# A new order, new engine choices and new buffer slots for a two-layer attention and MLP program

## The chip, the cores and the metric

The kernel runs on one core of a Trainium2 chip. The metric is the device time of one execution in microseconds. Of the core's engines, TensorE (PE, with its weight loads PEld) multiplies matrices into PSUM; VectorE (DVE), ScalarE (ACT) and GpSimd (POOL) do the elementwise work; SyncE (SP) issues DMAs. Each engine takes its own instructions in the order in which the program emits them, and waits on semaphores for the others.

## The reference

Two layers, each an attention part A and an MLP part B, both added to the residual, on x of 2048 rows by 512, all bfloat16:

```python
def A(x, wqkv, w_phi, wo):          # 32 heads of 16
    q, k, v = heads(x @ wqkv)
    pq, pk = q @ w_phi, k @ w_phi                     # per head
    phi_q = concat(softmax(pq), softmax(-pq))         # 32 features
    phi_k = concat(softmax(pk), softmax(-pk))
    kv, z = phi_k.T @ v, phi_k.sum(rows)
    o = (phi_q @ kv) / (phi_q @ z + 1e-6)
    return merge(o) @ wo
def B(x, W_gate, W_up, W_down):     # 512 -> 1376 -> 512
    return (relu(x @ W_gate) * (x @ W_up)) @ W_down
for _ in range(2):
    x = x + A(layernorm(x), ...)
    x = x + B(layernorm(x), ...)
```

## The kernel before

The 2048 rows are 16 tiles of 128. Everything stays on the chip: the residual X, the weights, and 21 buffers `ek` for exponentials. The program is a list of 1880 operations (`op`), each with an engine, what it waits for, and the buffers that it takes. An operation may have an alternative on another engine (`alt`).

At the start the key and query weights are multiplied by w_phi on PE ("fold", L448), after turning them: wk by PE (L440), wq by DMA transposes on SP (L435). In each layer a tile then goes through these steps; the line is that of the profile.

- Attention norm: statistics (L477), aggregate (L478), two small activations, scaling (L495), and a transpose to xnTA, by DMA on SP (L461) or by PE (L466) with a copy (L425).
- Keys: K on PE (L535), two exponentials (L538), V on PE (L541) with a copy to vext (L425 on ScalarE, L426 on VectorE), sums of 16 (L546), their reciprocal by two activations (L555, L558), the scaling of ek in two halves (L509, on VectorE or GpSimd), and the key-value sums on PE (L570), which all 16 tiles add into one PSUM tile.
- Queries: Q (L597), exponentials (L600), sums (L603), reciprocal (L606, L608), scaling in two halves (L509), and a DMA transpose to fq on SP (L611).
- Attention: R from the key-value sums (L582, L587), then per tile L622 on PE into the PSUM tile q, a reciprocal (L631 on VectorE, or L629 and L633 on ScalarE), L636, a transpose to oT, the projection (L645), and the residual (L649).
- MLP: centring (L665), square sum (L671 or L673), transpose to xnTB, the last columns of gate and up (L698), gate and up (L722) with relu (L726) and the product (L739 directly from PSUM, or L741 and L730), the down projection (L762), the residual (L769). The tiles go in blocks of 1 to 4. The output is stored by SP (L833).

No scheduler runs when the kernel is built: `arrange` reads the order from a list of numbers, and tables that were found offline say the rest. `PLACE` has a digit for each operation with an alternative (1: take it), `SLOTS` the buffer that each taking operation gets, `ORDER` the numbers of the operations in the order of emission, and `IDLE` how many dummy matmuls stand ahead of each PE operation. `arrange` asserts that an operation comes after those it depends on and that a buffer is free.

Of the kernel before, what the change touches and what calls it, by code (L numbers as in the profile page):

```python
# [142 lines left out]
class K:  # L143
# [9 lines left out]
    "0101110100000000001100000100110001000011010001111000000011001101010101001001001000101001111111011010"  # L153
    "1011110000000100000001001101000000000111011001011111010111000101001100000101111101001100001101010100"
    "1111111110101010010001000011000100000000101100101010100001001100011100010000110011001101000110111001"
    "010110010110111001110100110100000"
)
SLOTS = (
    "0001425210034050000151131234202310332121143404550125d3104c02302b3020a12113g533004002394131703202e141"
    "5i022124504f013k03583226105214413624335a011h100b033c05053623122j214910170400020501131002000245011020"  # L160
    "2500001142021002010100203200101143020002012105002004314023104g13300215112012320410311e34110200400450"
    "10205113120513d5100i42221240121321402422031200151030231042100142131004133610104f33242541002510104203"
    "51101520500512052130201550414201515300804024k2232c4020121152143124212004023502a533344112050010024104"
    "02024213011055002220j4203h05133317362b222f1506242i013a114023391638231c343e352k221d014g10011500020514"
    "0010124302000012011021450000121302100024010021050012201000011011521101530431102000005112025421011101"
    "0213125200125020013101050032154203115143114220221100253415210511200211401013403005210402213013222420"
    "500210300512431510432512113015114024105320310110512400202"
)
IDLE = (
    0, 0, 0, 0, 0, 0, 0, 0, 0, 0, 2, 0, 4, 0, 0, 0, 0, 0, 0, 0, 0,  # L170
# [11 lines left out]
    0, 24, 16, 3, 25, 17, 18, 20, 1, 4, 29, 22, 19, 21, 23, 26, 2, 5, 28, 6, 7, 46, 8, 9, 47, 48, 10, 49, 30, 50,  # L182
    11, 27, 32, 31, 36, 12, 51, 34, 37, 38, 13, 33, 39, 44, 35, 40, 14, 45, 42, 64, 15, 52, 82, 322, 43, 56, 41,
    100, 53, 65, 83, 57, 324, 101, 118, 102, 84, 120, 103, 66, 85, 54, 323, 104, 67, 86, 55, 105, 68, 87, 106, 119,
    121, 69, 58, 325, 122, 110, 70, 123, 88, 217, 71, 111, 124, 59, 89, 125, 60, 250, 72, 126, 61, 73, 252, 92, 90,
    76, 62, 91, 74, 93, 139, 253, 107, 251, 77, 184, 75, 127, 78, 219, 63, 254, 108, 80, 326, 186, 330, 255, 109,
    328, 256, 332, 331, 79, 187, 112, 329, 128, 333, 257, 113, 185, 81, 114, 94, 258, 188, 131, 129, 116, 130, 143,
    327, 95, 115, 271, 132, 151, 96, 140, 259, 189, 144, 97, 218, 220, 133, 221, 117, 222, 141, 98, 142, 153, 134,
    135, 190, 99, 191, 275, 137, 154, 145, 192, 272, 276, 223, 146, 205, 152, 363, 283, 147, 155, 193, 273, 148,
    285, 260, 156, 274, 284, 157, 364, 149, 286, 354, 277, 287, 261, 263, 288, 365, 158, 356, 289, 159, 150, 290,  # L190
    278, 206, 264, 262, 279, 355, 224, 209, 291, 281, 265, 207, 208, 194, 280, 210, 266, 225, 197, 267, 211, 195,
    268, 196, 173, 316, 198, 199, 269, 212, 161, 174, 213, 172, 136, 175, 176, 321, 200, 214, 162, 178, 138, 320,
    163, 296, 318, 201, 215, 179, 293, 317, 180, 297, 203, 166, 304, 216, 294, 292, 227, 181, 177, 295, 238, 336,
    167, 319, 298, 228, 182, 160, 168, 229, 305, 226, 337, 202, 408, 299, 169, 232, 306, 338, 282, 183, 300, 170,
    410, 339, 453, 233, 307, 302, 239, 234, 454, 310, 340, 345, 455, 235, 341, 366, 311, 240, 381, 342, 347, 230,
    456, 312, 382, 236, 367, 444, 241, 357, 231, 314, 270, 368, 445, 204, 308, 244, 457, 369, 358, 458, 346, 237,
    372, 383, 309, 370, 245, 446, 164, 343, 373, 371, 301, 374, 242, 246, 313, 409, 303, 165, 248, 375, 435, 359,
    344, 315, 247, 436, 243, 390, 437, 348, 360, 171, 376, 391, 249, 399, 377, 335, 392, 361, 349, 471, 379, 334,
    401, 362, 350, 384, 400, 426, 351, 473, 480, 472, 462, 352, 481, 427, 378, 353, 482, 417, 428, 483, 464, 429,
    418, 484, 380, 485, 463, 447, 486, 430, 385, 431, 419, 433, 488, 487, 448, 386, 489, 449, 490, 590, 587, 387,  # L200
    491, 588, 589, 496, 432, 492, 497, 598, 493, 388, 434, 498, 402, 599, 600, 389, 494, 499, 601, 403, 591, 602,
    595, 404, 495, 500, 406, 596, 614, 501, 502, 638, 597, 503, 603, 613, 635, 592, 405, 509, 605, 636, 504, 604,
    593, 393, 510, 637, 511, 608, 606, 512, 407, 643, 610, 609, 394, 594, 607, 644, 513, 395, 645, 611, 646, 474,
    396, 514, 515, 656, 661, 648, 397, 516, 657, 658, 507, 475, 659, 612, 517, 451, 476, 651, 477, 438, 647, 653,
    508, 439, 398, 505, 440, 450, 687, 441, 649, 652, 452, 506, 615, 650, 459, 684, 654, 662, 688, 683, 655, 520,
    685, 411, 686, 522, 663, 523, 660, 412, 521, 524, 413, 616, 414, 525, 764, 664, 617, 415, 526, 518, 618, 527,
    528, 478, 416, 695, 465, 705, 697, 479, 519, 466, 710, 707, 529, 761, 711, 760, 530, 712, 762, 619, 689, 639,
    696, 620, 442, 713, 640, 621, 690, 467, 420, 692, 698, 706, 763, 693, 699, 421, 694, 422, 535, 714, 708, 700,
    424, 536, 537, 720, 691, 538, 701, 702, 641, 622, 443, 423, 531, 703, 709, 642, 533, 704, 623, 460, 721, 665,
    425, 468, 725, 666, 722, 469, 461, 667, 627, 534, 668, 669, 532, 769, 470, 715, 670, 628, 765, 716, 717, 767,  # L210
    766, 671, 539, 770, 718, 624, 771, 540, 541, 772, 768, 719, 726, 542, 625, 773, 626, 723, 543, 629, 672, 675,
    724, 630, 673, 631, 729, 777, 674, 633, 676, 774, 778, 632, 544, 775, 677, 546, 545, 678, 548, 780, 679, 549,
    550, 910, 681, 825, 782, 551, 680, 815, 827, 547, 816, 817, 776, 779, 913, 826, 909, 830, 730, 911, 818, 781,
    828, 912, 819, 552, 727, 783, 553, 554, 795, 784, 829, 728, 796, 555, 797, 731, 556, 561, 800, 798, 562, 563,
    801, 799, 732, 802, 564, 733, 820, 734, 803, 805, 735, 822, 804, 736, 737, 557, 807, 559, 558, 806, 915, 914,
    560, 821, 918, 919, 916, 917, 808, 752, 920, 823, 921, 741, 809, 753, 824, 922, 810, 742, 811, 812, 749, 813,
    926, 814, 750, 565, 751, 929, 566, 567, 927, 754, 934, 931, 568, 755, 930, 936, 569, 756, 944, 757, 932, 574,
    933, 946, 785, 758, 575, 576, 577, 786, 787, 923, 788, 572, 924, 789, 925, 928, 790, 573, 979, 791, 1062, 792,
    578, 570, 579, 793, 580, 581, 945, 571, 582, 634, 935, 947, 1063, 1058, 759, 1059, 937, 738, 1060, 1064, 794,
    948, 938, 682, 1061, 739, 835, 1065, 1066, 740, 949, 743, 836, 951, 744, 831, 745, 746, 959, 747, 960, 961, 832,  # L220
    962, 843, 963, 969, 950, 971, 833, 952, 954, 834, 955, 953, 847, 956, 848, 974, 957, 975, 958, 976, 839, 977,
    978, 837, 840, 838, 844, 849, 850, 841, 851, 852, 845, 853, 854, 583, 842, 855, 846, 1070, 584, 1090, 1072, 880,
    1067, 1136, 1092, 585, 1135, 1068, 881, 878, 867, 1069, 586, 1095, 856, 879, 868, 1137, 1140, 882, 970, 1139,
    883, 857, 1141, 1071, 884, 972, 858, 869, 1091, 1142, 861, 748, 870, 973, 1143, 1093, 862, 863, 1073, 939, 871,
    864, 940, 941, 1094, 1074, 872, 964, 865, 873, 965, 874, 966, 942, 875, 1080, 943, 967, 1138, 885, 876, 980,
    1082, 968, 886, 992, 877, 1075, 1144, 1077, 1076, 1145, 1146, 887, 1078, 1079, 890, 888, 889, 1100, 891, 892,
    988, 984, 893, 894, 981, 895, 896, 985, 897, 982, 986, 983, 989, 987, 993, 996, 998, 990, 997, 999, 994, 1000,
    991, 1001, 1096, 1002, 995, 1147, 1027, 1152, 1172, 1029, 1149, 1028, 1003, 1148, 1154, 1030, 1004, 1031, 1153,
# [650 lines left out]
```

## Time and profile before

| what | before |
|---|---|
| median of three runs | 377.24 us (377.06 to 377.68) |
| span of the profiled execution | 375.3 us |
| the median less the span | 1.9 us |
| PE busy | 364.6 us, 97% |
| VectorE busy | 285.1 us, 596 instructions |
| ScalarE busy | 209.7 us, 553 instructions |
| GpSimd busy | 93.5 us, 91 instructions |
| granted TensorE clock | 1.00 |

The span runs from the first to the last instruction of the profiled execution; the time of a run has some 2 us more around it. The profile gives no time of its own for that execution beside the span. Busy times add up what lies side by side on different engines. An instruction's duration is longer than its spacing to the next one, since they overlap in the engine's pipeline: sums are made with the spacing. Line numbers are those of the kernel before; after the change all lines behind the tables are three lower.

### The profile page before, as it was taken

What the parts mean: (1) busy time and instruction counts of PE and PEld (TensorE: products, weight loads), DVE (VectorE), ACT (ScalarE), POOL (GpSimd) and SP (SyncE); (2) the same over time, 40 slices, a digit from 0 to 9 for tenths busy, and PEclk for the clock granted to TensorE, in tenths of its full rate; (3) what the DMA queues carried; (4) which work ended last, traced back from release to release, by engine and by line L of the source; (5) the groups of instructions that cost most, each with busy time, mean ns of one, the idle gap of its engine ahead of it and who ended that gap; (6) DMA issues with size and microseconds to landing.
All of it is one profiled execution on the core that took longest, in us unless ns stands there. A gap on an engine that the chain in (4) does not pass through costs nothing.

```text
span 375.3 us, 7459 instructions
## 1 busy us (share of the span) xinstructions
PE 364.6 (97%) x2793; PEld 216.6 (58%) x2833; DVE 285.1 (76%) x596; ACT 209.7 (56%) x553; POOL 93.5 (25%) x91
## 2 busy tenths in 40 slices
PE   8989997999999999999999999999999999999996
PEld 4534454868554554466476555587745444558585
DVE  6999999999998673685767999999994755543322
ACT  6989999746464532265155499973425323414031
POOL 0377984341010102001004269774000000000000
PEclk9999999999999999999999999999999999999999
DMA  8858844769814221012020102968664120211110
GB/s 256 191 139 175 312 58 85 123 113 132 164 36 84 47 53 31 11 25 56 9 56 2 29 2 57 141 93 142 143 132 85 31 56 2 56 29 51 42 51 30
DMA packets 93444, 31.21 MB, mean 83 GB/s; under 512 B 85248, under 2 KB 92384, under 8 KB 93408
## 3 DMA queue, kind: packets, MB, share of 16 engines
q1 hardware_dynamic: 92992, 30.34, 39.5%
q8 instruction: 22, 0.36, 0.4%
q10 hardware_dynamic: 416, 0.39, 0.3%
q14 instruction: 14, 0.11, 0.1%
HBM read 7.91 MB, written 2.10 MB: 27 GB/s over the span
## 4 chain that ended last, share of the span: by engine, by line
PE 90%; ACT 6%; DVE 1%; POOL 1%; issue 1%; DVEq 0%; another core or an unknown queue 0%
PE b L722 37%; PE b L762 20%; PE b L645 7%; PE b L541 6%; PE b L535 6%; PE b L597 6%; PE b L698 3%; PE q L622 2%; PE q L570 2%; ACT ek L600 1%; POOL ek L509 1%; ACT ek L538 1%; PE q L419 1%; DVE sq L603 1%; ACT hT L425 1%
## 5 line engine op out<-in xcount | busy, mean ns | idle before, releaser
L722 PE MATMUL b<-xnTB,wgu 128*128 128x128 bf16 (+2 forms) x1200 | 149.6, 279 | 0.0
L722 PEld LDWEIGHTS <-wgu 128*128 128x128 bf16 x1200 | 97.1, 98 | 43.6
L509 POOL TENSOR_TENSOR ek<-ek,sk 128x512 bf16<-128x512 bf16 x47 | 51.0, 1109 | 135.5 <-ACT sk L558 108.2
L726 ACT ACTIVATE gu<-b 128x512 bf16<-128x512 f32 (+1 forms) x83 | 47.8, 580 | 64.9 <-PE b L722 64.6
L762 PE MATMUL b<-wd,hT 128*128 128x512 bf16 (+2 forms) x350 | 81.3, 372 | 0.7
L762 PEld LDWEIGHTS <-hT 128*128 128x128 bf16 (+1 forms) x363 | 34.6, 98 | 35.9 <-DVE hT L739 0.2
L509 POOL TENSOR_TENSOR ek<-ek,sq 128x512 bf16<-128x512 bf16 x38 | 42.0, 1127 | 32.6 <-ACT sq L608 18.0
L739 DVE TENSOR_TENSOR hT<-gu,b 128x512 bf16<-128x512 bf16 (+1 forms) x44 | 29.6, 676 | 18.5 <-PE b L722 16.9
L546 DVE TENSOR_REDUCE sk<-ek 128x64 f32<-128x1024 bf16 x32 | 38.7, 1210 | 5.3 <-ACT ek L538 5.2
L538 ACT ACTIVATE ek<-b 128x512 bf16<-128x512 f32 x64 | 35.9, 598 | 9.2 <-PE b L535 8.0
L603 DVE TENSOR_REDUCE sq<-ek 128x64 f32<-128x1024 bf16 x32 | 38.2, 1207 | 0.3 <-POOL ek L509 0.3
L600 ACT ACTIVATE ek<-b 128x512 bf16<-128x512 f32 x64 | 36.1, 623 | 0.6 <-PE b L597 0.5
L730 DVE TENSOR_TENSOR hT<-gu 128x512 bf16<-128x512 bf16 (+1 forms) x39 | 16.7, 429 | 22.5 <-ACT gu L741 22.3
L769 DVE SCALAR_TENSOR_TENSOR X<-b,rsB,X 128x512 bf16<-128x512 f32 (+1 forms) x33 | 23.2, 726 | 13.5 <-PE b L762 13.4
L645 PE MATMUL b<-wo,oT 128*128 128x512 bf16 x118 | 31.2, 379 | 1.2 <-ACT oT L425 0.7
L535 PE MATMUL b<-Wk,xnTA 128*128 128x512 bf16 x122 | 31.4, 379 | 0.3
L541 PE MATMUL b<-wv,xnTA 128*128 128x512 bf16 x124 | 31.0, 379 | 0.4 <-ACT xnTA L425 0.2
L597 PE MATMUL b<-Wq,xnTA 128*128 128x512 bf16 x121 | 30.5, 379 | 0.3
L741 ACT CAST gu<-b 128x512 bf16<-128x512 f32 (+1 forms) x39 | 21.7, 558 | 15.0 <-PE b L722 14.6
L649 DVE SCALAR_TENSOR_TENSOR X<-b,X 128x512 bf16<-128x512 f32 x32 | 21.8, 682 | 3.5 <-PE b L645 3.4
L636 DVE TENSOR_TENSOR o<-q,rd 128x512 bf16<-128x512 f32 x32 | 21.9, 685 | 0.8 <-ACT rd L633 0.6
L477 DVE BATCH_NORM_STATS2 bstA<-X 128x6 f32<-128x512 bf16 x32 | 21.0, 681 | 1.9 <-DMA X<-in_A_x_dram 1.8
(71 smaller groups left out, 349.1 us busy)
## 6 DMA issues: line engine op xcount, KB each, us to landing
out_dram<-X SPq DMA_DIRECT2D x15, 128.0 KB, 1.7
X<-in_A_x_dram SPq DMA_DIRECT2D x6, 256.0 KB, 4.8
wgu<-in_B_W_gate_dram SPq DMA_DIRECT2D x4, 344.0 KB, 4.0
wgu<-in_B_W_up_dram SPq DMA_DIRECT2D x4, 344.0 KB, 3.6
wd<-in_B_W_down_dram SPq DMA_DIRECT2D x5, 256.0 KB, 3.6
wv<-in_A_wqkv_dram SPq DMA_DIRECT2D x2, 256.0 KB, 4.3
wo<-in_A_wo_dram SPq DMA_DIRECT2D x4, 128.0 KB, 3.2
fq<-ek SPq DMA_TRANSPOSE x32, 3.3
```

The source lines that it names most:

```text
L509: e.tensor_tensor(out=out().rearrange("p g s (h f) -> p (g s h) f", f=DH)[:, lo:lo + n], in0=ek.t[:].rearrange("p g s (h f) -> p (g s h) f ...
L535: k = op("PE", mm(4, 512), due, lambda: [nc.tensor.matmul(kp.t[:], lhsT=xnTA[c][:, i, b, :], rhs=Wk2[:, b, :], start=(b == 0), stop=(b == ...
L538: e = [op("ACT", act(512), due, lambda s=s: nc.scalar.activation(out=ek.t[:, :, s, :], in_=kp.t[:].rearrange("p (g e) -> p g e", e=GQ), fu ...
L541: v = op("PE", mm(4, 512), due_v, lambda: [nc.tensor.matmul(vp.t[:], lhsT=xnTA[c][:, i, b, :], rhs=wv[:, b, :], start=(b == 0), stop=(b == ...
L546: a = op("DVE", SUM16, due, lambda: nc.vector.tensor_reduce(out=sk.t[:, row, :], in_=ek.t[:].rearrange("p g s (h f) -> p (g s h) f", f=DH) ...
L597: q = op("PE", mm(4, 512), due, lambda: [nc.tensor.matmul(qp.t[:], lhsT=xnTA[c][:, i, b, :], rhs=Wq2[:, b, :], start=(b == 0), stop=(b == ...
L600: e = [op("ACT", act(512), due, lambda s=s: nc.scalar.activation(out=ek.t[:, :, s, :], in_=qp.t[:].rearrange("p (g e) -> p g e", e=GQ), fu ...
L603: a = op("DVE", SUM16, due, lambda: nc.vector.tensor_reduce(out=sq.t[:], in_=ek.t[:].rearrange("p g s (h f) -> p (g s h) f", f=DH), axis=A ...
L645: a = op("PE", mm(4, 512), due + 3, lambda j=j, yp=yp: [nc.tensor.matmul(yp.t[:], lhsT=oT.t[:, j, b, :], rhs=wo[:, b, :], start=(b == 0), ...
L722: nc.tensor.matmul(ps.t[:, q * W:(q + 1) * W].rearrange("p (i t) -> p i t", t=P), lhsT=wgu[:, s, b, g * P:(g + 1) * P], rhs=xT.t[:, 0:n, b ...
L726: nc.scalar.activation(out=gu.t[:, 0, 0:cols], in_=gp.t[:, 0:cols], func=AF.Relu)
L762: nc.tensor.matmul(yp.t[:, 0:c1 - c0], lhsT=h.t[:m, f * W + i * P:f * W + (i + 1) * P], rhs=wd[:m, f, c0:c1], start=(f == 0), stop=(f == N ...
```

## The change

Only the four tables are replaced, all else is the same text. They were found anew on a model of the machine that knows a lock between the SBUF ports of VectorE and GpSimd and takes all events in order of time. The diff, cut:

```diff
 PLACE = (
-    "0101110100000000001100000100110001000011010001111000000011001101010101001001001000101001111111011010"
...
+    "0101010100000000001100000000111000000110100010001000000000010100000000000001000000000000000010001010"
...
 IDLE = (
-    0, 0, 0, 0, 0, 0, 0, 0, 0, 0, 2, 0, 4, 0, 0, 0, 0, 0, 0, 0, 0,
+    0, 2, 0, 1, 0, 0, 0, 0, 3, 0,
...
 ORDER = (
-    0, 24, 16, 3, 25, 17, 18, 20, 1, 4, 29, 22, 19, 21, 23, 26, 2, 5, 28, 6, 7, 46, 8, 9, 47, 48, 10, 49, 30, 50,
...
+    0, 3, 25, 20, 18, 19, 24, 2, 17, 16, 4, 21, 29, 9, 26, 8, 22, 23, 1, 28, 7, 10, 46, 14, 47, 30, 48, 322, 32, 49,
...
```

Numbers 3 to 15 are loads, 322 to 325 the DMA transposes of wq, 29 the warming matmuls, 30, 32, 34 and 36 the turning of wk. What the tables mean on the engines, counted in the two built programs:

| operation | before | after |
|---|---|---|
| key scaling halves (L509) | VectorE 17, GpSimd 47 | VectorE 20, GpSimd 44 |
| query scaling halves (L509) | VectorE 26, GpSimd 38 | VectorE 12, GpSimd 52 |
| value copies | VectorE 13, ScalarE 19 | VectorE 7, ScalarE 25 |
| gate times up | L739 44, L741 and L730 39 | L739 39, L741 and L730 44 |
| reciprocals in attention | VectorE 17, ScalarE 15 | VectorE 14, ScalarE 18 |
| square sums | VectorE 11, ScalarE 21 | VectorE 8, ScalarE 24 |
| folded weight copies | VectorE 2, ScalarE 6 | VectorE 1, ScalarE 7 |

PE has the same operations, in another order: ahead of the first key-value sums (L570) stand 4 V, 4 K and 4 folds before, and 6 V, 7 K and all 8 folds after; five queries of the second layer stand in the middle of the first layer's MLP. On SP the wq transposes stand among the loads of X instead of behind them, and two of the late weight loads stand ahead of the last X loads.

## The prediction

> **What bounds the kernel now.** I read the page's busy shares and slices first, then PE's waits, then the timeline around the longest of them, then VectorE's groups.
>
> ```profile
> PE 364.6 (97%) x2793; PEld 216.6 (58%) x2833; DVE 285.1 (76%) x596; ACT 209.7 (56%) x553; POOL 93.5 (25%) x91
> ...
> PE   8989997999999999999999999999999999999996
> ...
> DVE  6999999999998673685767999999994755543322
> ACT  6989999746464532265155499973425323414031
> POOL 0377984341010102001004269774000000000000
> PEclk9999999999999999999999999999999999999999
> ```
>
> PE is the wall, but a busy PE need not run at its peak, so I counted its work. Matmuls with nothing between them start 0.216 us apart for 512 columns, 0.109 for 256, 0.083 for 192, 0.056 for 128 and 0.032 for the 65 and 68 wide ones: 1187, 422, 128, 584 and 512 of them make 256.4 + 46.0 + 10.6 + 32.7 + 16.4 = 362 us, dummies included. The rest of the 375.3 is PE's delay: the time at which a group starts less the PE work issued before it. Read off the timeline, the delay is 1.3 us at the first matmul, 4.9 at 13 us, 7.2 at 28 us, 9.8 at 64 us and 10.1 at 365 us. Two stretches make the last 4.9 us, and nothing after 64 us makes more than 0.3. Between 14 and 64 us PE waited for:
>
> ```profile
> PE q L570 <- POOL ek L509: 1.5, 3, 0.7
> PE b L466 <- DVE xn L665: 0.8, 1, 0.8
> PE b L645 <- ACT oT L425: 0.7, 1, 0.7
> PE q L622 <- DVE o L636: 0.2, 1, 0.2
> PE b L466 <- DVE o L636: 0.2, 1, 0.2
> ```
>
> The first line is 18 to 25 us (start gaps 2.3 us in all): key-value sums whose scaled keys GpSimd has not finished. The others are 59 to 64 us (2.6 us): the first tile's way from attention to the MLP.
>
> ```profile
> 59.75 2.33 DVE L603 TENSOR_REDUCE sq<-ek 128x64 f32<-128x1024 bf16 x2
> 59.88 0.40 PE L466 MATMUL b<-ident,o 128*128 128x128 bf16 x4 [0.17 <-DVE o L636]
> 60.95 1.04 PE L645 MATMUL b<-wo,oT 128*128 128x512 bf16 x4 [0.68 <-ACT oT L425]
> ...
> 62.77 0.35 DVE L665 TENSOR_SCALAR xn<-X,rowsum 128x512 bf16<-128x512 bf16 x1
> ...
> 63.18 0.40 PE L466 MATMUL b<-ident,xn 128*128 128x128 bf16 x4 [0.84 <-DVE xn L665]
> ...
> 63.77 0.42 PE L622 MATMUL q<-R,fq 128*128 128x68 bf16 x8 [0.20 <-DVE o L636]
> ```
>
> VectorE runs two L603 reductions for later queries while PE needs it for the first tile. Its groups from 5 to 63 us show 1.3 us idle in all, so what it finishes when is the sum of what is queued ahead:
>
> ```profile
> L546 DVE TENSOR_REDUCE sk<-ek 128x64 f32<-128x1024 bf16 x16 | 19.3, 1209 | 0.1
> L603 DVE TENSOR_REDUCE sq<-ek 128x64 f32<-128x1024 bf16 x9 | 10.6, 1206 | 0.0
> ...
> L509 DVE TENSOR_TENSOR ek<-ek,sq 128x512 bf16<-128x512 bf16 x4 | 3.2, 816 | 0.0
> ```
>
> **The change part by part.** The operations are the same 1880, and PE's are the same to the matmul (six dummies in both), so PE's 362 us stay. Moved are engines, places in the queues, and buffers.
>
> *Engine choices.* Counted in the two built programs: query scalings (L509) on VectorE 26 to 12, on GpSimd 38 to 52; key scalings on VectorE 17 to 20, on GpSimd 47 to 44; value copies (L426/L425) on VectorE 13 to 7, on ScalarE 19 to 25; up-projections read directly by VectorE 44 to 39; three reciprocals, three square sums and one weight copy leave VectorE as well. By spacings in this trace (0.60 us for a 512-wide product, reading or copy, 0.34 for the L730 product, 0.27 for a reciprocal, 0.61 for a square sum) VectorE sheds 11 x 0.60 + 6 x 0.60 + 5 x (0.60 - 0.34) + 3 x 0.27 + 3 x 0.61 + 0.60 = 14.7 us. ScalarE gains 6 + 5 + 1 readings at 0.48, three pairs at 0.22 and three square sums at 0.63: 8.3 us. GpSimd gains 11 x 1.02 = 11.2 us. None of this is a saving by itself; it counts where PE waits.
>
> *Order before 64 us.* I take the third L622 group, which waits for the second tile's L636. VectorE's queue up to that L636, before: 16 statistics x 0.60, 16 aggregates x 0.09, 16 normalisations x 0.32, 25 reductions x 1.13, 20 products and copies x 0.60, one L649 and L665 0.87, small ones 1.1: 58.4 us. Measured end 63.7, so VectorE's own start and idling are 5.2 us. PE has 54.0 us of work before it, and 58.4 + 5.2 + 0.1 - 54.0 = 9.7, the delay that the trace shows (9.8). After: 24 reductions and 16 products and copies, since one L603, three value copies and a weight copy stand later or elsewhere: 54.9 us, against 54.2 of PE. With the same 5.2 the delay is 6.0. The first L622 asks more: VectorE's sum through L582 and L587 is 49.9 against PE's 48.7, and with the 5.0 us that VectorE had idled by then the delay is 6.3.
>
> *ScalarE.* The first L722 group needs the L425 copy of xnTB: sum ahead 54.6 before, 51.9 after (25 query exponentials stand ahead of it, not 32). ScalarE's start and idling were 9.4 us there; kept whole, the delay would be 51.9 + 9.4 + 0.1 - 54.4 = 7.0. Part of that idling was waiting for VectorE's reductions, so 7.0 is the upper end.
>
> *Bare latency.* With every engine free, the first tile's path still takes L645 1.03, L649 0.69 and L665 0.35, and PE has 1.9 us of other work there after the change and 1.1 before; the copy to xnTB (0.6 behind 0.4 us of transposes) leaves 0.3 us uncovered in both. So 6.3 plus 0.3 to 0.6. Between 6.3 and 7.0 I take 6.9, the ScalarE end being the nearer row. What is late next is then PE itself.
>
> *Start.* ScalarE's table load (1.28 us) now stands ahead of its weight load, a Wq fold (L448) stands ahead of the first K and waits for a DMA transpose, and on SP the Wq transposes stand among the X loads, while the load of tiles 14 and 15 waits behind an xnTA transpose. Before, such a transpose landed 4.0 us after issue; now the first is eighth on SP, issued near 0.7 + 7 x 0.53 = 4.5 us, and lands near 9, and PE is held until about 10 anyway by the Wk copies, then by tile 3 (L495 near 10.3). K71 comes at about 12.9 with 7.7 us of PE work ahead, delay 5.2 (4.9 before). Tiles 14 and 15 land near 19 to 20 us, their statistics come up near 21.5. A gain below 4.9 is not to be had here, a loss of 1 us is.
>
> *Key-value sums.* The first L570 stands after 17.8 us of PE work instead of 12.6; GpSimd's first product then starts near 15.3 (14.5 before), and at the closest L570 its sum is 11.6 us under PE's; with the 16.2 us that GpSimd had lost at 25 us before, that asks for a delay of 4.6. The 2.3 us wait goes; the 6.3 above takes its place in part.
>
> *From 64 us.* PE had nothing to give back there, so this part can only lose. Five second-layer query groups stand at 97 to 160 us of PE work (none before 207 in the old order), and at the first L622 of the second layer VectorE's sum less PE's falls from 188.2 - 224.7 = -36.5 to 180.4 - 226.4 = -46.0, so it has 9 us more room there. I cost it at nothing; the cover is that room, and it is gone if a single bank or buffer is short (first rival).
>
> Sum: 9.8 - 6.9 = 2.9 us off the 375.3 us span, 372.4. The runs' median is 1.9 us above the span: 374.3.
>
> **GpSimd and the port.** Beside VectorE's L509, GpSimd's products stretch:
>
> ```profile
> 37.67 6.06 POOL L509 TENSOR_TENSOR ek<-ek,sk 128x512 bf16<-128x512 bf16 x5 [0.39 <-ACT sk L558]
> 41.12 0.68 DVE L509 TENSOR_TENSOR ek<-ek,sk 128x512 bf16<-128x512 bf16 x1
> ```
>
> Five undisturbed ones take 5.1 us; 16 of 85 ran over 1.1 us, up to 1.57, 5 us together. The Trainium skill, page "SBUF — State Buffer", section "Who interferes with whom", says that a VectorE instruction with two SBUF inputs and a GpSimd one that reads SBUF exclude each other, the later one blocking whole; the trace agrees (1.57 against 1.06). By it the stretch should shrink, VectorE having 32 such L509 instead of 43. Against the change speaks "GPSIMD Engine Reference", section "Engine selection": elementwise products belong on VectorE, GpSimd being about twice as slow. The trace agrees on the price, 1.02 against 0.60 us; by that rule alone 14 moved products would cost 14 x 0.42 = 5.9 us.
>
> **Rivals.**
> *Narrow banks.* Six PSUM banks pass between PE and its readers. Counting PE work between a bank's last matmul and its next use, less the reader's 0.60 us and 0.2 of signalling, 15 places behind 64 us have under 0.1 us to spare, 2 before. If ScalarE is in a 0.48 us instruction at four in ten of them, that is 15 x 0.4 x 0.48 = 2.9 us: the gain is eaten, 377.2. For it: ScalarE has 8 us more to do. Against: outside 215 to 265 us it is 35 to 60% busy, and a free ScalarE takes the reader at once.
> *GpSimd late (slower).* The first L622 needs transposed queries behind 28.3 us of GpSimd work. Before, GpSimd reached that sum with 21.4 us of start, idling and stretch: 49.7, plus 3.3 for the DMA transpose, 53.0. PE comes at 48.7 + 6.3 = 55.0. Room 2.0 us. If the products nearly all meet the lock, 14 more at 0.5 us make 60.0, a delay of 11.3 against 9.8, and 378.7. It decides when GpSimd loses 2 us more than before, and it is a loss from 5.5 us more. For it: 11 more products, packed. Against: fewer two-input products on VectorE, and GpSimd waits less, its reductions being earlier in VectorE's queue. The engine-selection rule points here.
> *Better.* ScalarE's idling shrinks with VectorE's queue and the start costs nothing: delay 5.7, 373.1.
> That the change does not do what it says is excluded by the built queues.
>
> **Chances.** Forecast 0.64 (own range 373.4 to 375.8), better 0.06, narrow banks 0.15, GpSimd or the start late 0.15. Three runs spread by 0.16%, so 0.2%, 0.75 us, is what can be told from no change. Faster: 0.64 + 0.06 and 0.06 of the banks' case, 0.76. Same 0.08, slower 0.16. Range 373.0 to 377.6: it leaves out the far ends of GpSimd late and better.
>
> **What would show it.** Right: PE's delay 5 to 5.5 at 13 us, no L570 wait on GpSimd between 18 and 25, about 6.9 when the first L722 starts (near 61.5 us), flat after that. Wrong: L622 or L645 waits near 55 us naming the DMA fq or GpSimd; L722 waits on ScalarE after 64 us; a delay over 7 already at 15 us.

## The result, and the profile after

The changed kernel takes 376.37 us (median of 20 runs, 375.47 to 377.99), the old one beside it 377.53 (20 runs, 376.99 to 377.74): a ratio of 0.9978, 95% interval 0.9969 to 0.9986. It is faster by 1.16 us, where 2.9 had been forecast. The profiled execution took 375.65 us (span 373.5); the old one's span was 375.3.

Lines of the changed kernel's own profile are three lower than those of the kernel before (L506 is the old L509). The experiments from e3 on were written in the old layout and have the old numbers. First the page:

```profile
PE 364.0 (97%) x2787; PEld 216.4 (58%) x2833; DVE 272.3 (73%) x569; ACT 211.7 (57%) x577; POOL 103.9 (28%) x102
...
PE   7999999999999999999999999999999999999996
...
DVE  6999999996896696658987959997885554143333
ACT  5999999745348743385345677884434426322211
POOL 0296967871000322001402184645100000000000
PEclk9999999999999999999999999999999999999999
```

VectorE sheds 12.8 us and GpSimd gains 10.4, near the 14.7 and 11.2 of the prediction. PE stays the wall. Its waits between 14 and 64 us:

```profile
PE b L532 <- DMA xnTA<-xn: 0.5, 1, 0.5
PE b L463 <- DVE o L633: 0.2, 1, 0.2
```

The three L570 waits on GpSimd (1.5 us) and the waits on xn and oT (0.8 and 0.7 us) are gone; a new one on a DMA transpose has come. PE's timeline around the first tile's way to the MLP shows why the old waits are gone:

```profile
56.66 0.39 PE L463 MATMUL b<-ident,o 128*128 128x128 bf16 x4
56.88 1.03 PE L594 MATMUL b<-Wq,xnTA 128*128 128x512 bf16 x4
57.74 1.03 PE L642 MATMUL b<-wo,oT 128*128 128x512 bf16 x4
58.61 0.42 PE L619 MATMUL q<-R,fq 128*128 128x68 bf16 x8
58.86 1.02 PE L594 MATMUL b<-Wq,xnTA 128*128 128x512 bf16 x4
60.02 0.40 PE L463 MATMUL b<-ident,xn 128*128 128x128 bf16 x4
```

A query group (L594) now stands on each side of the projection (L642), while ScalarE copies oT and VectorE makes X and xn. Before, PE had none there. PE's delay (start of a group less the PE work issued before it, as in the prediction) goes like this. The first two rows are the profiles shown, the next two are the same changed kernel profiled twice more (e1, e2). The last two columns are the span of the profiled execution and the time of the same execution:

| profile | at 13 us | near 28 | near 61 (before, e2: 64) | 228 | end | span | time |
|---|---|---|---|---|---|---|---|
| before | 4.9 | 7.2 | 9.8 | 9.8 | 10.1 | 375.3 | not known |
| after | 5.1 | 5.8 | 6.7 | 6.95 | 8.4 | 373.5 | 375.65 |
| after, e1 | 5.1 | 5.85 | 6.7 | 7.0 | 8.3 | 373.4 | 375.59 |
| after, e2 | 5.5 | 7.2 | 8.1 | 8.4 | 9.9 | 375.1 | 377.23 |

Three things stand out. The 3.1 us that the first profile has won at 61 us shrink to 1.7 at the end: from there on the delay rises by 1.7 us, in the old kernel by 0.3, and 1.3 to 1.5 of it come in behind 228 us, in all three profiles. In e2 the delay is 1.4 us larger from 28 us on, and it is carried to the end whole, so nothing behind it has room to give back. And the time outside the span has grown: a run of the changed kernel takes 2.10 to 2.27 us more than its own span (20 runs), one of the old kernel 1.74 to 1.86 (51 runs beside the experiments). That takes some 0.35 us off the gain, in every run.

### The profile page after: what moved, and what is told of

Same layout as the page of the kernel before. It is cut to its first block, busy times and chain, and to the rows that moved or that the text cites. A ratio compares the mean times of both kernels' runs of the same rounds, so it can differ in the third digit from the quotient of the medians.

```text
span 373.5 us, 7407 instructions
## 1 busy us (share of the span) xinstructions
PE 364.0 (97%) x2787; PEld 216.4 (58%) x2833; DVE 272.3 (73%) x569; ACT 211.7 (57%) x577; POOL 103.9 (28%) x102
## 4 chain that ended last, share of the span: by engine, by line
PE 83%; ACT 7%; DVE 5%; issue 2%; DMA 2%; POOL 1%; DVEq 0%
PE b L719 37%; PE b L759 19%; PE b L642 7%; PE b L532 5%; PE b L538 5%; PE b L695 3%; PE b L594 3%; ACT ek L535 2%; DVE ek L506 2%; PE q L619 2%; PE q L567 2%; PE q L416 1%; ACT ek L597 1%; DMA xnTA<-xn 1%; DMA xnTB<-xn 1%
## 5 line engine op out<-in xcount | busy, mean ns | idle before, releaser
L719 PE MATMUL b<-xnTB,wgu 128*128 128x128 bf16 (+2 forms) x1200 | 153.3, 279 | 0.2
L719 PEld LDWEIGHTS <-wgu 128*128 128x128 bf16 x1200 | 97.7, 98 | 47.9 <-issue 0.3
L759 PE MATMUL b<-wd,hT 128*128 128x512 bf16 (+2 forms) x344 | 84.2, 372 | 0.8
L506 POOL TENSOR_TENSOR ek<-ek,sk 128x512 bf16<-128x512 bf16 x44 | 46.3, 1078 | 111.6 <-ACT sk L555 109.1
L506 POOL TENSOR_TENSOR ek<-ek,sq 128x512 bf16<-128x512 bf16 x52 | 57.4, 1130 | 47.0 <-ACT sq L605 34.1
L736 DVE TENSOR_TENSOR hT<-gu,b 128x512 bf16<-128x512 bf16 (+1 forms) x39 | 25.3, 653 | 27.3 <-ACT gu L723 19.7
L535 ACT ACTIVATE ek<-b 128x512 bf16<-128x512 f32 x64 | 37.5, 617 | 6.5 <-PE b L532 6.3
L597 ACT ACTIVATE ek<-b 128x512 bf16<-128x512 f32 x64 | 36.6, 622 | 2.4 <-PE b L594 2.4
L727 DVE TENSOR_TENSOR hT<-gu 128x512 bf16<-128x512 bf16 (+1 forms) x44 | 19.1, 441 | 25.5 <-ACT gu L738 25.5
L642 PE MATMUL b<-wo,oT 128*128 128x512 bf16 x119 | 31.1, 379 | 0.5
L594 PE MATMUL b<-Wq,xnTA 128*128 128x512 bf16 x121 | 31.1, 379 | 0.4
L738 ACT CAST gu<-b 128x512 bf16<-128x512 f32 (+1 forms) x44 | 24.9, 577 | 11.7 <-PE b L719 11.7
```

Of the source, the lines that this page charges most:

```text
L506: e.tensor_tensor(out=out().rearrange("p g s (h f) -> p (g s h) f", f=DH)[:, lo:lo + n], in0=ek.t[:].rearrange("p g s (h f) -> p (g s h) f ...
L535: e = [op("ACT", act(512), due, lambda s=s: nc.scalar.activation(out=ek.t[:, :, s, :], in_=kp.t[:].rearrange("p (g e) -> p g e", e=GQ), fu ...
L594: q = op("PE", mm(4, 512), due, lambda: [nc.tensor.matmul(qp.t[:], lhsT=xnTA[c][:, i, b, :], rhs=Wq2[:, b, :], start=(b == 0), stop=(b == ...
L597: e = [op("ACT", act(512), due, lambda s=s: nc.scalar.activation(out=ek.t[:, :, s, :], in_=qp.t[:].rearrange("p (g e) -> p g e", e=GQ), fu ...
L642: a = op("PE", mm(4, 512), due + 3, lambda j=j, yp=yp: [nc.tensor.matmul(yp.t[:], lhsT=oT.t[:, j, b, :], rhs=wo[:, b, :], start=(b == 0), ...
L719: nc.tensor.matmul(ps.t[:, q * W:(q + 1) * W].rearrange("p (i t) -> p i t", t=P), lhsT=wgu[:, s, b, g * P:(g + 1) * P], rhs=xT.t[:, 0:n, b ...
```

## The experiments

**e1 and e2: the changed kernel again.** No edit.

> The changed kernel itself, unaltered, profiled once more. Lock theory: PE's delay is again about 6.7 us at 61 us and flat to 223 us (that part is fixed by the order of the queues), while VectorE products (L506) that meet a GpSimd product stretch in other places or by other amounts than in the first profile, since who holds the port depends on tenths of a microsecond; the step at 239.5 us may be 0 to 0.9 us, the delay at the end 7.6 to 9, the span 372.8 to 375. Queue theory (VectorE simply has too much queued ahead of the first xn of the second layer): the step of 0.75 us at 239.5 us comes again in the same size, also where L506 at 237 us is not stretched.

> The changed kernel once more, as the run before: with three profiles of the same program, differences in PE's delay at the end can be traced to the place where they arise. Lock theory: at a place where a VectorE L506 is stretched in one run and not in the other. Queue theory: no differences over 0.2 us at such places.

Measured: 375.59 and 377.23 us. My lock theory of the spread is wrong: the same VectorE products stretch by the same amounts in all three profiles. Of the 1.4 us between e2 and the first profile, 0.3 to 0.4 are there at 13 us, and the rest arises at 20 to 27 us. PE's waits of e2 there are these; the first profile had only 0.5 us for xnTA:

```profile
PE b L532 <- DMA xnTA<-xn: 0.8, 1, 0.8
PE b L532 <- ACT ek L535: 0.7, 1, 0.7
```

The first names a DMA transpose, the second is put down to ScalarE's exponentials. SP's queue in e2 shows what the transposes stood behind (start, time to issue):

```profile
15.01 3.50 SPq L432 DMA_TRANSPOSE hT<-in_A_wqkv_dram  x2
18.56 0.58 SPq L345 DMA_DIRECT2D wd<-in_B_W_down_dram  x1
19.23 1.90 SPq L458 DMA_TRANSPOSE xnTA<-xn  x1
21.18 0.58 SPq L345 DMA_DIRECT2D wd<-in_B_W_down_dram  x1
21.86 1.23 SPq L458 DMA_TRANSPOSE xnTA<-xn  x1
```

Each of these two transposes stands behind a 256 KB load of wd, which is not needed before 63 us, and the first took 1.90 us to issue (1.23 in the first profile). That is tried in e5. The step of 0.75 us at 239.5 us came three times in the same size, in e2 at 1.4 us more delay. VectorE's L506 ahead of it stood as much later in e2 (238.4 against 236.9 us) and was stretched every time, so these runs tell neither a queue from a latency nor either from the lock.

**e3: the new first part, the old second.** `ORDER` and `PLACE` of the changed kernel up to operation 598 (the first up-projection), the old ones for all that is left.

```diff
 ORDER (the changed kernel's) ..., 588, 589, ..., 598,
-    then the changed kernel's order
+    then the old kernel's order of what is left
```

> The changed kernel's queues and engine choices up to the first down-projection of the first layer (61 us), the old kernel's behind it; buffers reassigned. Lock theory (the gain up to 61 us is whole, and what is given back arises behind 223 us from VectorE and GpSimd meeting in the new order of the second layer): delay 6.7 us at 61 us, no step over 0.3 behind it, 7.0 to 7.3 at the end, 374 to 374.6 us, ratio 0.990 to 0.993. Rival (the early gain is eaten later by any order, since the old second part was bound by VectorE or by banks that need the larger delay): the delay climbs back to 8.3 or more in the first 40 us behind 61, 375.5 to 377 us.

Measured: 380.99 us, ratio 1.010 (1.008 to 1.012). The delay is 7.4 at 61 us (6.5 at 23, after a wait of 1.4 us ahead of the K group at which the other runs wait for xnTA), and then PE's waits show 3.4 us in one place:

```profile
PE q L622 <- DVE o L636: 3.4, 1, 3.4
```

TensorE then ran at half speed for a while. The row of the granted clock in e3's page, whose slices are 9.5 us long:

```profile
PEclk9999999899999999999999999999999999999999
```

The trace has a granted clock of 0.5 from 69.1 to 72.6 us, right behind that wait. The delay rises by some 3.6 us at the wait and by another 1.7 in this stretch; all six runs have a mean granted clock of 0.991 to 0.996.

The old second part asks for a third attention tile at once, and the new first part has left its query work for later (VectorE's reduction for it waits 1.53 us for ScalarE's exponentials). That speaks for a gain at 61 us that is partly work put off, and that holds only with a PE order behind it that does not need this work yet. Both expectations missed the time; of the rival's, the delay over 8.3 us within 40 us came. Behind this place the old second part adds 0.5 us from 88 us to the end, where the changed one adds 1.5, but at a delay of 13.5 us that says little on the late give-back.

**e4: the GpSimd product moved back two places.**

```diff
 GpSimd's queue at 234 us
-    1262, 1361, 1261, 1270, 1271
+    1262, 1261, 1270, 1271, 1361
```

The DMA transpose that reads this product (1362, on SP) moves back with it.

> The changed kernel with one GpSimd product of the second layer moved behind the next two in GpSimd's own queue, so that GpSimd does not run beside VectorE's L506 at 237 us; VectorE's, ScalarE's and PE's queues are the same. Lock theory: that L506 takes 0.68 us and not 1.57, PE's wait for xn at 239.5 us (0.75 us of delay) goes, delay at the end 7.6 for 8.4, ratio to the old kernel 0.995 to 0.997. Queue theory: the wait of about 0.75 us stays, since VectorE's queue is the same, ratio 0.998.

Measured: 378.21 us, ratio 1.0026 (1.0012 to 1.0039). VectorE's product took 0.68 us, and the step at 239.5 us was 0.3 and not 0.75, as the lock theory said. But 2 us more came right behind: VectorE's second reduction after it waited 1.62 us for GpSimd, as it takes the small scale buffer that product 1361 still holds. (This run's start was also among the late ones, 7.5 us of delay at 28.)

**e5: the transposes first.**

```diff
 SP's queue at 15 us (316, 317: wd loads; 258, 192: xnTA transposes)
-    325, 324, 316, 258, 317, 192, 319
+    325, 324, 258, 192, 316, 317, 319
```

> The changed kernel with two loads of the down-projection's weights (wd, 256 KB each, not needed before 63 us) moved on SP from just before the last-but-few xnTA transposes to just behind them. In three profiles of the changed kernel and of one near copy, PE's delay after the K groups of 22 to 27 us was 5.8, 5.85, 7.2 and 7.5 us, and all that came after was carried to the end whole. Theory (SP's queue and the loads' traffic make the two transposes late): no wait on xnTA over 0.2 us between 20 and 28 us, delay 5.3 to 5.5 us at 28 us in every run, spread of the times halved, about 375.2 us, ratio 0.993 to 0.995. Rival (the transposes are late by VectorE's normalisations, or by traffic of other loads): delay still 5.8 to 7.5 us at 28 us, ratio 0.997 to 0.999.

Measured: 375.15 us (374.67 to 375.93), ratio 0.9944 (0.9931 to 0.9958). The waits on xnTA are gone; of PE's waits from 14 to 64 us only this is left:

```profile
PE b L466 <- DVE o L636: 0.2, 1, 0.2
```

The delay was 4.9 at 28 us, 5.8 at 61 and 7.4 at the end. So the places of two loads on SP cost the changed kernel 1.2 us in the median. The spread of e5's five runs is 1.3 us, that of the changed kernel's 20 runs 2.5. The expected size was right; the delay at 28 us is lower than expected, the start having been an early one.

**e6: VectorE's product behind the residual.**

```diff
 VectorE's queue at 236 us (1360: L506 product; 1370: residual; 1471: xn)
-    1374, 1360, 1370, 1471, 1285
+    1374, 1370, 1471, 1360, 1285
```

> The changed kernel with VectorE's L506 product of 237 us moved two places back in VectorE's queue, behind the residual (L646) and the normalisation (L662) that PE waits for. Lock theory: the residual starts when its projection is done, about 0.2 to 0.45 us sooner than in the changed kernel, the product meets no GpSimd product and takes 0.68 us; step at 239.5 us 0.3 us instead of 0.75, ratio 0.996 to 0.998 (0.45 us better than the changed kernel at the same delay before). Rival (the product's own consumers need it: SP's fq, the buffer that its group gives back): VectorE or PE waits on them within 15 us, and the delay at 260 us is as large as before or larger.

Measured: 377.10 us, ratio 0.9989 (0.9980 to 0.9999). The product took 0.68 us and the step was 0.3 us, but what the rival says of the delay came: VectorE idled 0.94 us waiting for the projection, all behind came later, and PE waited 0.6 us for a transposed o at 250 us. From 228 us to the end 2.0 us of delay came in (1.4 in the changed kernel). Of the two places tried, the one where the product stood is the better, but for the lock.

**e7: one GpSimd product left out.** One half of one query group of the second layer stays unscaled.

```diff
-            o.emit()
+            if o is not ops[1261]:
+                o.emit()
```

> The changed kernel with one instruction left out: the GpSimd product of 236.9 to 237.9 us (one half of one group of query features of the second layer stays unscaled). Nothing else moves, and PE does not wait for GpSimd near there. Lock theory: VectorE's L506 of 237 us takes 0.68 us and not 1.57, and PE's step at 239.5 us is 0.3 us or less, not 0.75; the steps behind 249 us stay. Queue theory: L506 is short or long, the step of 0.75 us stays.

Measured: 374.99 us, a single run. GpSimd's timeline in the changed kernel at this place (three products in one row):

```profile
234.38 3.53 POOL L506 TENSOR_TENSOR ek<-ek,sq 128x512 bf16<-128x512 bf16 x3 [3.55 <-ACT sq L605]
```

VectorE's timeline beside it:

```profile
236.89 1.57 DVE L506 TENSOR_TENSOR ek<-ek,sq 128x512 bf16<-128x512 bf16 x1
238.38 0.68 DVE L646 SCALAR_TENSOR_TENSOR X<-b,X 128x512 bf16<-128x512 f32 x1
...
239.10 0.35 DVE L662 TENSOR_SCALAR xn<-X,rowsum 128x512 bf16<-128x512 bf16 x1
```

PE's timeline, the wait that follows:

```profile
239.51 0.40 PE L463 MATMUL b<-ident,xn 128*128 128x128 bf16 x4 [0.37 <-DVE xn L662]
```

And VectorE's timeline in e7:

```profile
236.66 0.68 DVE L509 TENSOR_TENSOR ek<-ek,sq 128x512 bf16<-128x512 bf16 x1
237.68 0.69 DVE L649 SCALAR_TENSOR_TENSOR X<-b,X 128x512 bf16<-128x512 f32 x1 [0.34 <-PE b L645]
```

GpSimd's run of three ends at 237.91; the last of them began at 236.85, 0.04 us before VectorE's product, which then took 1.57 us. Without it, it takes 0.68, and the residual waits for PE and not PE for the residual. The step is 0.29 us instead of 0.75. From 228 us to the end the delay rises by 1.0 us instead of 1.4. The lock is thus 0.45 us of the late give-back, shown by taking away nothing but the neighbour. The other 1.0 us are small steps of 0.1 to 0.4 us between 238 and 310 us: the largest stand at 255.6, 259.7 and 272.6 us. PE's weight loads in the changed kernel, from 238 to 312 us, name a wait at the first two, the DMA transposes of xn and of o:

```profile
PEld L642 <- DMA oT<-o: 0.3, 1, 0.3
PEld L719 <- DMA xnTB<-xn: 0.2, 1, 0.2
```

These steps were not tested one by one, and what makes the transposes late stays open, as do the causes of the others.

**e8: the new order with the old engine choices.** `PLACE` of the old kernel in the changed one.

> The changed kernel's order with the old kernel's engine choices (11 more query products, 6 more value copies and some smaller work back on VectorE). By sums of what is queued ahead, VectorE's work less PE's at 57 us of PE work is 3.9 us instead of 1.0, and 6.4 at 76 us: with VectorE's 5.2 us of start and idling the delay is 9 us at 60 us and 11.5 at 80, 378 to 380 us, ratio 1.001 to 1.007. Rival (the order alone brings the gain, the engines only follow): delay 7 us at 60 us, 376 us.

Measured: 399.44 us, ratio 1.057 (1.055 to 1.059). The delay at the first transposes of xn is 13.7 us and not 9. The sum of the queues gave 9.1; what it left out is the lock, as VectorE's groups from 5 to 64 us show (0.68 us is undisturbed):

```profile
L509 DVE TENSOR_TENSOR ek<-ek,sk 128x512 bf16<-128x512 bf16 x5 | 5.0, 1014 | 0.0
...
L509 DVE TENSOR_TENSOR ek<-ek,sq 128x512 bf16<-128x512 bf16 x3 | 3.2, 1072 | 0.0
```

These products and three normalisations lose some 4.2 us to GpSimd up to 61 us (each instruction's duration less the undisturbed one of its form), and 9.1 + 4.2 is 13.3, near the 13.7 measured. So a sum over VectorE's queue comes near only if the lock is added, and it has to be read off for each order. Behind this place the delay goes on rising, to 24 us at 228 and 32 at the end; why was not followed.

**e9: both mends.** e5, and GpSimd's product 1361 moved one place less far than in e4.

```diff
 GpSimd's queue at 234 us, on top of e5
-    1262, 1361, 1261, 1270, 1271
+    1262, 1261, 1270, 1361, 1271
```

> The changed kernel with the two wd loads behind the xnTA transposes, as in the run before that did only this (375.15 us), and with one GpSimd product (the one of 235.4 to 236.9 us) moved behind the next but one, into a gap in which GpSimd idles 1.3 us or more: the product that it feeds is read at 278 us only. GpSimd then stands idle when VectorE's product of 236 us runs. Lock theory: that product takes 0.68 us, the step at 238.6 us is 0.3 and not 0.75, delay at the end 7.0 us (7.5 without the second edit), 374.7 us, ratio 0.992 to 0.994. Rival (as when the same product was moved one place further: the small buffer of its reciprocal comes free too late and VectorE waits 1.6 us for it): a VectorE wait on GpSimd at 241 us, delay at the end 8 us or more, 375.7 us or more.

Measured: 376.50 us, ratio 0.9979 (0.9970 to 0.9988), worse than e5. The step at 239 us is 0.3 us, but the rival's wait came, with a third of e4's wait among VectorE's waits:

```profile
DVE sq L603 <- POOL ek L509: 0.6, 1, 0.6
```

From 228 us to the end the delay rises by 2.1 us. The start was 1.0 us later than in e5's profile as well, which led to e11.

**e10: the old order with the new engine choices.** `PLACE` of the changed kernel in the old one.

> The old kernel's order with the changed kernel's engine choices, the other half of the change by itself. By sums of what is queued ahead, VectorE's work less PE's at the third attention group (54 us of PE work) is 1.4 us (old kernel 4.4, changed kernel 1.0), ScalarE's at the first up-projection 2.0 (0.2 and -2.1). Sums alone: delay 6.6 us by VectorE, up to 11.4 by ScalarE if it idles as long as in the old kernel (9.4 us); taken 8 to 9, 376 us. Lock theory, from the run with the new order and the old engines: an order and engine choices that were not found together meet the lock more often; each us by which VectorE's products stretch before 64 us comes on top (there 4.3 us, so up to 13 us, 380 us). If the delay at 64 us is under 7 us, the order adds nothing.

Measured: 391.26 us, ratio 1.040 (1.036 to 1.045). The delay is 15.5 at the third attention group, above all that I had given (11.4, or 13 with the lock); where the difference comes from was not followed. Old order, old engines: 377.2 to 377.6 us; new order, new engines: 376.4; the mixed ones: 391 and 399. In both mixed kernels the buffers and the dummies go with the order. Neither half of the change is a gain by itself.

**e11 and e12: the dummies at the start.** The first lines of PE's timeline in the old kernel:

```profile
1.34 3.60 PE L419 MATMUL q<-zero 128*128 128x512 bf16 x8 [1.34 <-DVE zero L396]
4.72 0.90 PE L440 MATMUL b<-ident,hT 128*128 128x128 bf16 x12
```

In the changed kernel:

```profile
1.38 3.95 PE L416 MATMUL q<-zero 128*128 128x512 bf16 x10 [1.38 <-DVE vext L395]
5.17 0.61 PE L437 MATMUL b<-ident,hT 128*128 128x128 bf16 x8
```

And in e9:

```profile
1.38 4.45 PE L419 MATMUL q<-zero 128*128 128x512 bf16 x10 [1.38 <-DVE vext L398]
5.62 0.99 PE L440 MATMUL b<-ident,hT 128*128 128x128 bf16 x8
```

The changed kernel has ten dummies and not eight ahead of the first weight transposes, and these run at 0.427 us each until TensorE has reached full speed.

```diff
 IDLE (on top of e5; e12 also has idle(6) for idle(8) in the warming matmuls)
-    0, 2, 0, 1, 0, 0, 0, 0, 3, 0,
+    0, 0, 0, 1, 0, 0, 0, 0, 5, 0,
```

> The run with the two wd loads behind the transposes (375.15 us), and the two dummy matmuls that the changed kernel has ahead of its first weight transposes (L440) moved behind the last of them, to three others, where PE waits for ScalarE. Seen in the profiles so far: TensorE starts at half speed (0.427 us for a dummy instead of 0.216) and reaches full speed between 4.2 and 6.5 us, in another place in each run; ten dummies ahead of the first transpose end at 4.87 to 5.62 us, the old kernel's eight at 4.72 to 4.75, and the weights landed near 4.0. Theory (these dummies are the rest of the start's loss and of the spread): first transpose at 4.7 to 4.8 us in every run, K at 10.0 or before, delay 4.6 to 4.8 at 13 us, 374.6 to 374.9 us, spread of the runs under 1 us. Rival (the start is bound by ScalarE's copies or the X tiles, so that two dummies cost nothing): 375.1 us, spread as before.

> As the run beside it, and with six warming dummies instead of eight ahead of the first transposes (two matmuls of a constant less, nothing of the result). Theory: the first transpose starts when the weights have landed, near 4.0 us, 0.7 us sooner; the chain from there to the first K is copies on ScalarE, so K comes 0.3 to 0.7 us sooner too, 374.1 to 374.6 us. Rivals: the first tile's normalisation and its transpose (near 6.3 us) hold K where it is, and nothing is won, 374.7 us; or PE, less busy before 4 us, reaches full speed later, and the transposes and folds at half speed eat the gain, 375 us or more.

Measured: e11 374.88 us (374.59 to 375.38), ratio 0.9940 (0.9926 to 0.9953); e12 374.94 us (374.75 to 375.03), ratio 0.9938 (0.9926 to 0.9951). Against e5 the gain is 0.2 to 0.3 us, inside the intervals. The spread is 1.3 us in e5's runs, 0.8 in e11's and 0.3 in e12's; with five runs each that is a hint and no more. e11's profile caught a late full speed (5.5 us) and still has 5.0 us of delay at 13 us, where e9 with ten dummies and full speed at 6.4 us had 5.8. In e12 the transposes start at 4.02 us, as expected, but K comes only 0.08 us sooner (9.94 us, 10.02 in e11). Just ahead of it PE waits 0.24 us for a normalised xn (L495; 0.32 in e11), which is what the first rival says, only of a later tile. The second rival is not excluded: e12 reached full speed at 6.6 us, and its first fold (L448) took 0.58 us instead of 0.40. e5, e11 and e12 beat both kernels, the old one by 2.3 to 2.4 us.

## Why the prediction was right and wrong

*Up to 61 us: right.* Forecast was a delay of 6.9 us, 5 to 5.5 at 13 us, no L570 wait on GpSimd, and flat behind; measured 6.7, 5.1, none, and 6.7 to 7.0 up to 228 us. The number came by a way that only half held: I had VectorE's queue and ScalarE's copy set it. In fact e5, with the same VectorE queue, stands 0.9 us lower at 61 us, because it was that much lower at 28. From 28 to 61 us the delay rises by 0.9 us in the four rows e5, after, e1 and e2, whatever it was before. So the delay at 61 us goes by the start, and VectorE's queue alone was no longer the bound. It was not far from one: from 28 to 61 us VectorE was busy for 32.2 of the 33 us in the changed kernel and for 32.5 in e5. What the 0.9 us are made of was not taken apart.

*"I cost it at nothing" (from 64 us): the step that failed most.* 1.4 us of the 3.1 were given back: the delay rises by 1.7 us from 61 us to the end, and by 0.3 in the old kernel. The cover that I named, 9 us more room in VectorE's sum, does not help: a sum tells whether an engine is late on average, and not whether one result comes in time. At 239.5 us PE waits for the first tile's way from the projection through X and xn, where a product that GpSimd blocks stands in between. 0.45 us are this lock (e7). Of the rest, two steps near 256 and 260 us, together 0.4 us, are waits for DMA transposes by the trace; no run tested them. What causes the remainder, most of it between 238 and 310 us, stays open.

*The port.* I used the rule of the Trainium skill, page "SBUF — State Buffer", section "Who interferes with whom", for GpSimd's products alone and expected the stretch to shrink. It did there, by little (over 1.06 us each, from 4.8 to 4.4 us in all), and grew on VectorE. VectorE's groups of before:

```profile
L509 DVE TENSOR_TENSOR ek<-ek,sq 128x512 bf16<-128x512 bf16 x26 | 19.1, 744 | 0.0
L509 DVE TENSOR_TENSOR ek<-ek,sk 128x512 bf16<-128x512 bf16 x17 | 11.8, 708 | 1.2 <-ACT sk L558 1.2
```

And of after:

```profile
L506 DVE TENSOR_TENSOR ek<-ek,sk 128x512 bf16<-128x512 bf16 x20 | 15.4, 796 | 0.9 <-ACT sk L555 0.9
L506 DVE TENSOR_TENSOR ek<-ek,sq 128x512 bf16<-128x512 bf16 x12 | 10.1, 848 | 1.4 <-ACT sq L605 1.4
```

Over 0.68 us each, VectorE's 43 products lost 26 x 0.064 + 17 x 0.028 = 2.1 us before, and its 32 lose 20 x 0.116 + 12 x 0.168 = 4.3 us now. That section of the Trainium skill says that whoever issues first has the port and the other blocks fully, on either engine. The measurement agrees (1.57 us, and 0.68 in e7); I read it for one engine only.

*The start: "a loss of 1 us is" to be had.* It was named as a bound and left out of the value. The wait for the xnTA transposes came, of 0.5 to 1.9 us in the profiles that have this start (after, e1, e2, e4, e6, e7), and the median run is 0.7 us slower than the profiled one (376.37 against 375.65); that this wait and the dummies make the difference is what e5 and e11 speak for. I had added the old kernel's 1.9 us between span and median. That term was too small twice: it cannot carry a spread that the old kernel does not have, and the time outside a run's own span grew from 1.8 to 2.15 us. Why it grew no run shows. The mixed kernels e3, e8 and e10 have the old 1.8, all other variants of the changed kernel 2.07 to 2.24.

Together: -2.9 forecast, the first part 0.2 better and 1.4 given back late make -1.7 between the two profiles, whose spans differ by -1.8. The medians stand 2.9 us above the profiled span now and 2.2 in the old kernel's 20 runs; of these 0.6 us, 0.35 are the time outside the span and the rest is the spread. That makes -1.1. The measured 376.37 lies in the range given, and outside the forecast's own (373.4 to 375.8).

*The rivals.* "Narrow banks" gave 377.2, not far from the result, but its mechanism does not show: no wait of PE on ScalarE at L719 stands among the waits, and the late steps that the trace names are waits for VectorE or for DMA transposes. "GpSimd late" did not occur either: no PE wait on fq or GpSimd near 55 us; moved onto GpSimd, the products cost nothing on PE's path, only the lock did. "Better" had a free start for a condition; e5 and e11, with the start mended, reach a delay of 5.8 to 6.0 at 61 us, near its 5.7, and miss its 373.1, mostly by the late give-back.

## What to carry to other kernels

A gain on a wall of busy time is kept only where nothing later needs it: follow the delay of the bound engine over the whole span, and look for latencies with too little cover wherever the order has changed, even where every sum has room. Where two engines exclude each other, add the blocked time on both, for the very order that runs: here the new engine choices in the old order cost 14 us, and the old ones in the new order 22. Before anything late is touched, look at what each queue carries ahead of the first critical transposes; two loads moved by two places gave as much as the whole change.

## What the runs showed of the hardware

- TensorE's way to full speed took another time in each run. In the fourteen profiles the dummies' spacing fell from 0.427 to 0.216 us, or the transposes' from 0.107 to 0.056, between 4.1 and 6.6 us, 2.7 to 5.2 us after the first matmul. The profile's row of the granted clock does not show it, since a slice of it is 9 us long. The Trainium skill, page "TensorE: Matmul & The Clock Gate", section "Part 1: The HAM clock gate", tells of half speed until some 4 us of activity, at a moment that varies with a free-running window; these runs agree on the spacings, and their range is wider than the ±0.5 us given in its "What you observe".
- The lock takes VectorE's single-input normalisations too: with a GpSimd product just before it, an xn took 0.90 us in e9 instead of 0.35. The Trainium skill, page "SBUF — State Buffer", section "Who interferes with whom", names such operations among those that can enter the two-port mode and then contend with GpSimd; the trace agrees.
- Full speed was lost again behind a pause of PE. In e3 a wait of 3.4 us is followed by a granted clock of 0.5 from 69.1 to 72.6 us, in e8 one of 2.3 us by the same from 275.9 to 279.3; the delay rises by another 1.7 and 1.6 us in these stretches. It is not so in every run: one of e8's four had a mean granted clock of 1.000, and took 397.76 us where the others, at 0.996, took 399.1 to 399.8.
- A product that starts 0.04 us behind one of GpSimd's lost 0.9 us, nearly all of that one's 1.06.
